# Merged attention posts and a hand-set first batch in a fused RWKV6 and MLP-mixer kernel

## Chip, cores and metric

The kernel runs on one core of one Trainium2 chip. The metric is device time in microseconds (us) of one execution. A kernel's time is the median of several executions; where two kernels are compared, both ran on the same chip in the same rounds. The granted clock is the share of TensorE's full clock that the profile says was granted. All executions that are quoted here count as fast, but for one of the kernel before: at 700.29 us it is 1.6% above that kernel's fastest (689.36), counts as slow and is left out.

## What is computed

Two blocks in float32. The first is a linear-attention recurrence over 768 tokens, for 4 batches of 8 heads of width 48; its output, heads side by side, is the 384-wide input of a mixer with a token MLP (768 to 256 to 768) and a channel MLP (384 to 1536 to 384).

```python
for t in range(S):                                    # attention, per batch and head
    cur = einsum('bhd,bhe->bhde', u[None] * kt, vt)
    y[:, :, t] = einsum('bhd,bhde->bhe', rt, state + cur)
    state = wt[:, :, :, None] * state + einsum('bhd,bhe->bhde', kt, vt)
# mixer
h  = maximum(xt @ w_tok1, 0) @ w_tok2                 # xt: tokens last
u  = x + h.transpose(0, 2, 1)
h2 = maximum(u @ w_ch1, 0) @ w_ch2
return u + h2
```

The four weight matrices arrive as float64, and the kernel itself turns them into float32 on VectorE.

## The kernel before

A batch is three *units* of 256 tokens, a unit two *chunks* of 128. A unit's attention has two halves. `levels` builds the token-by-token weights within 64 tokens in six doubling steps (on TensorE a *gram* of 32 products, which the trace shows as 64 instructions, then *joins* of k, r and w on VectorE and *picks* of the wanted results on VectorE or ScalarE). `post` carries the state: transposes of k, products kv, a state update on VectorE, then y. The *mixer* of a batch is token products (`hidden`, `back`), transposes (`turn`) and, per segment of 256 tokens, `up` and `down` products. Attention of batch n+1 is woven into the mixer of batch n: `woven` mixes lists of pieces in proportion to their estimated costs. During the mixer of batch 0 all weights still have to be converted.

```python
def emit(pieces):                       # the scheduler may reorder what is emitted
    for _, f in pieces:
        f()
...
def convert(dst, src):                  # one piece of float64 weights, six VectorE steps in a chain
    sp.dma_start(d64..., src)           # d64: 2 buffers
    act.activation(size, hi, AF.Abs)
    dve.tensor_scalar(cut, hi, ...)
    dve.scalar_tensor_tensor(cut, hi, ..., cut)
    dve.tensor_scalar(scale, cut, ...)
    dve.scalar_tensor_tensor(low, lo, ..., low)        # low is scale
    dve.tensor_add(low, low, cut)
    dve.scalar_tensor_tensor(dst, size, NORMAL, low, ...)
...
# post(i): for each of the two chunks c of a unit
#   tokens(c): 4 transposes, one copy       carry(c): kv tile of 1 buffer, then the state updates
#   before(c): y from the state              within(c): y from the weights, copy to x
return pieces + [(0.01, lambda: load_rkw(i + 3)), (0.01, lambda: load_v(i + 3))]
...
def up(s, jt):
    if jt == 0:
        zs[s] = mpool.tile([128, NJ, SEG], f32, name="z")          # 2 buffers
    ps = ps_m.tile([128, SEG], f32, name="z_ps", tag="m")          # ps_m: 2 buffers
    ...
def down(s, n, jts=range(NJ)):
    if jts[0] == 0:
        sums[s, n] = ps_m.tile([128, DM], f32, name="h2_ps", tag="m")
    ...
# batch 0
emit(woven(levels(0), levels(1)))
...
emit(woven(levels(2), p0 + p1, to_tok1))
emit(woven(p2[:-4], to_tok2[:2]))
emit(p2[-4:-2] + hiddens[4] + p2[-2:] + hiddens[5])
emit(woven(turned, to_tok2[2:] + to_ch1[:3]))
both = [f for e in zip(ups[0], ups[1]) for f in e]
emit(woven(both, to_ch1[3:] + to_ch2[:6]))
emit(woven(downs[0][:-4], to_ch2[6:]))
pieces = downs[0][-4:] + ups[2] + downs[1] + downs[2]   # then woven with the attention of batch 1
```

Whole units of the next batch may thus be pulled forward by the scheduler into gaps of the weight conversions: nothing but data dependencies and buffers forbids it.

## Time and profile before

| | before |
|---|---|
| median of 3 runs (range) | 690.79 us (689.36 to 692.17) |
| span of the profiled run, mean granted clock | 685.6 us, 0.978 |
| last state add of batch 0 (VectorE) | 76.94 us |
| last weight ready (start of the last conversion's last operation, plus its length) | 183.91 us |
| first token product of batch 1, 2, 3 (TensorE) | 254.76, 411.83, 566.82 us |

The last three rows are markers that I read off the engines' timelines, each from one profiled execution. That execution lay up to 3.2 us from its kernel's median (here 687.6 us against 690.79), so a difference of 2 or 3 us between markers of two kernels shows nothing. I call the last weight's time **W** and the first token product of batch 1 **B1**. The lines on what bounds the kernel are in the prediction. The following were not shown there: what VectorE waited for in the first 190 us of the kernel before (total us, times, longest us).

```profile
DVE k L250 <- PE gram L225: 8.2, 11, 1.5
DVE k L250 <- DMA w<-in_rkw_dram: 5.2, 1, 5.2
DVE state L306 <- PE kv_ps L296: 3.0, 2, 2.4
```

No wait of a conversion is among them, and the longest wait of any kind is 5.2 us.

### The profile page before, as it was taken

The page shows a single profiled execution, that of the slowest core. Times are in us where ns is not written, and L with a number is a line of the kernel's source. Part 1 is how long each engine was busy: PE and PEld are TensorE (multiplying, and loading weights), DVE is VectorE, ACT ScalarE, POOL GpSimd, SP SyncE. Part 2 cuts the span into 40 slices and gives each one's busy share as a digit, 9 for nine tenths or more (in the row PEclk, how much of TensorE's full clock was granted, in tenths as well). Part 3 has the DMA queues.
Part 4 walks back from the last instruction along what each step waited for, and adds up shares of the span by engine and source line. Part 5 has one row for each costly group of instructions (what it writes and reads, how often), then busy time and mean ns, then how long its engine had stood idle before and what let it go on. Part 6 is the DMA issues. An engine that isn't in the chain of part 4 may idle for free.

```text
span 685.6 us, 18835 instructions
## 1 busy us (share of the span) xinstructions
PE 641.6 (94%) x8584; PEld 466.9 (68%) x8584; DVE 293.1 (43%) x585; ACT 194.8 (28%) x489; POOL 7.2 (1%) x32
## 2 busy tenths in 40 slices
PE   3889998996799999999999999999999999999998
PEld 3877656863586666788677656788677655786854
DVE  5998899998821435442242305442132211000000
ACT  7144533441242123432321303432211201220200
POOL 3000000000000000000000000000000000000000
PEclk9997898998899999999999999999999999999999
DMA  9244544332202131110210312000000000000000
GB/s 345 69 107 132 146 140 126 124 115 71 70 25 81 36 95 48 25 25 5 80 35 3 94 35 60 2 2 2 13 13 2 25 12 12 1 0 12 12 16 31
DMA packets 16111, 38.56 MB, mean 56 GB/s; under 512 B 2176, under 2 KB 8320, under 8 KB 16032
## 3 DMA queue, kind: packets, MB, share of 16 engines
q1 hardware_dynamic: 15888, 37.36, 17.9%
q8 instruction: 67, 1.10, 0.7%
q14 instruction: 12, 0.10, 0.0%
q10 hardware_dynamic: 144, 0.00, 0.0%
HBM read 32.64 MB, written 4.72 MB: 54 GB/s over the span
## 4 chain that ended last, share of the span: by engine, by line
PE 87%; DVE 9%; issue 2%; ACT 1%; DMA 1%; SPq 0%; DVEq 0%; ACTq 0%
PE z_ps L375 29%; PE h_ps L384 28%; PE gram L225 9%; PE h_ps L353 5%; PE h_ps L360 5%; PE y_ps L331 4%; PE kv_ps L296 2%; PE y_ps L318 2%; DVE r L251 1%; DVE k L250 1%; PE kT_ps L284 1%; PE gram L211 1%; PE xT_ps L367 1%; DVE at L217 1%; DMA w<-in_rkw_dram 1%
## 5 line engine op out<-in xcount | busy, mean ns | idle before, releaser
L375 PE MATMUL z_ps<-xT,wch 128*128 128x256 f32 x864 | 203.2, 389 | 3.5 <-DVE wch L161 3.0
L384 PE MATMUL h_ps<-wch,z 128*128 128x384 f32 x576 | 198.6, 498 | 3.7 <-DVE wch L161 3.5
L375 PEld LDWEIGHTS z_ps<-xT,wch 128*128 128x128 f32 x864 | 161.4, 192 | 28.4 <-DVE wch L161 3.2
L384 PEld LDWEIGHTS h_ps<-wch,z 128*128 128x128 f32 x576 | 107.9, 192 | 73.1 <-DVE wch L161 3.7
L377 ACT ACTIVATE z<-z_ps 128x256 f32<-128x256 f32 x144 | 55.1, 383 | 177.3 <-PE z_ps L375 177.2
L225 PEld LDWEIGHTS gram<-r,k 48*64 48x64 f32 x3840 | 76.5, 152 | 34.7 <-issue 24.3
L225 PE MATMUL gram<-r,k 48*64 48x32 f32 x3840 | 85.2, 235 | 13.1 <-DVE r L251 8.5
L388 DVE TENSOR_TENSOR o<-x,h_ps 128x384 f32<-128x384 f32 x24 | 13.3, 554 | 181.9 <-PE h_ps L384 181.9
L250 DVE TENSOR_TENSOR k<-k,decay 112x512 f32<-112x512 f32 x36 | 24.9, 691 | 62.2 <-PE gram L225 62.2
L242 ACT COPY at<-gram 16x256 f32<-16x256 f32 (+1 forms) x72 | 31.2, 434 | 44.7 <-PE gram L225 37.3
L250 DVE TENSOR_TENSOR k<-k,w 112x512 f32<-112x512 f32 x36 | 24.8, 688 | 39.6 <-PE gram L225 32.9
L360 PE MATMUL h_ps<-h,wtok 128*128 128x384 f32 x96 | 36.0, 503 | 1.8 <-DVE x L362 1.8
L353 PE MATMUL h_ps<-x,wtok 128*128 128x384 f32 x96 | 37.0, 520 | 0.0
L331 PEld LDWEIGHTS y_ps<-vt,at 64*64 64x64 f32 x768 | 26.2, 142 | 9.9 <-ACT seen L324 6.3
L234 DVE COPY_PREDICATED at<-mask,gram 128x512 f32<-128x512 uint8 x36 | 32.3, 897 | 0.0
L251 DVE TENSOR_TENSOR r<-r,w 112x512 f32<-112x512 f32 x36 | 24.7, 686 | 16.5 <-ACT rp L195 16.5
L331 PE MATMUL y_ps<-vt,at 64*64 64x48 f32 x768 | 29.2, 227 | 2.1 <-ACT seen L324 1.8
L211 PE MATMUL gram<-rp,kp 48*64 48x64 f32 x768 | 20.1, 246 | 11.1 <-ACT kp L199 8.0
L211 PEld LDWEIGHTS gram<-rp,kp 48*64 48x64 f32 x768 | 17.1, 154 | 16.4 <-ACT kp L199 10.4
L217 DVE COPY_PREDICATED at<-mask,gram 128x512 f32<-128x512 uint8 x24 | 16.7, 725 | 25.7 <-PE gram L211 25.4
L155 ACT ACTIVATE size<-d 128x384 f32<-128x384 f32 (+1 forms) x28 | 17.0, 608 | 28.2 <-DMA d<-in_w_ch_dram 13.3
L324 ACT COPY seen<-y_ps 64x2 f32<-64x2 f32 x44 | 6.8, 154 | 63.6 <-PE y_ps L318 63.3
(50 smaller groups left out, 429.1 us busy)
## 6 DMA issues: line engine op xcount, KB each, us to landing
vt<-in_v_dram SPq DMA_DIRECT2D x12, 384.0 KB, 3.9
d<-in_w_ch_dram SPq DMA_DIRECT2D x9, 512.0 KB, 3.6
d<-in_w_ch_dram SPq DMA_DIRECT2D x12, 384.0 KB, 3.0
out_dram<-o SPq DMA_DIRECT2D x24, 192.0 KB, 1.9
w<-in_rkw_dram SPq DMA_DIRECT2D x18, 192.0 KB, 3.5
k<-in_rkw_dram SPq DMA_DIRECT2D x18, 192.0 KB, 3.5
r<-in_rkw_dram SPq DMA_DIRECT2D x18, 192.0 KB, 3.4
r<-in_rkw_dram SPq DMA_DIRECT2D x3, 512.0 KB, 6.1
```

What stands on the lines that cost most here:

```text
L211: pe.matmul(g[cols, q, ts(a, T)], L["kp"][rows, tokens], L["rp"][rows, tokens], start=True, stop=True)
L225: fours(lambda q, j, rows, cols: pe.matmul(g[cols, q, ts(ca, 32)], k_[rows, ds(ca * 128 + j * T, T)], right[rows, ts(2 * ca + j, 32 // b), ...
L234: dve.copy_predicated(out=dst, data=g.rearrange("p q (m b) -> p q m b", b=b), mask=masks[l].rearrange("p x t -> p (x t)").rearrange("p (m ...
L242: act.copy(at[p:p + b, :, :, n * 2 * b + b:(n + 1) * 2 * b], g[p:p + b, :, :, ts(n, b)])
L250: dve.tensor_mul(left, left, wv[:, :, 1].unsqueeze(2).to_broadcast([ROWS, n, b]))
L251: dve.tensor_mul(right, right, wv[:, :, 0].unsqueeze(2).to_broadcast([ROWS, n, b]))
L331: pe.matmul(y[ts(j, T), q, ts(a, D)], at[ts(j, T), q, c * A + a, :], vt[ts(j, T), c, ts(2 * a + q, D)], start=(2 * ch + j == 0 and a == A ...
L353: pe.matmul(sums[i], wtok1[:, c, ts(i, 128)], xs[bt][:, c, :], start=(c == 0), stop=(c == C - 1))
L360: pe.matmul(ps, wtok2[:, i, ts(c, 128)], h1[:, i, :], start=(i == 0), stop=(i == DTOK // 128 - 1))
L375: pe.matmul(ps, wch1[:, m, ts(jt, 128)], xT[:, m, ts(s, SEG)], start=(m == 0), stop=(m == DM // 128 - 1))
L377: act.activation(zs[s][:, jt, :], ps, AF.Relu)
L384: pe.matmul(ps, zs[s][:, jt, ts(n, 128)], wch2[:, jt, :], start=(jt == 0), stop=(jt == NJ - 1))
```

## The change

Its intent: in `post`, both chunks of a unit go through one kv tile and one y tile, so that TensorE's work comes in four blocks instead of eight. In batch 0, the order of TensorE, VectorE, ScalarE and SyncE is set by hand (`fixed=True`), units staggered, with dummy products meant to keep TensorE fast; the three weight-conversion stages are fixed too.

```diff
+    def emit(pieces, fixed=False):
+        for _, f in pieces:
+            ...                         # each TensorE, VectorE, ScalarE, SyncE instruction is put
+            ...                         # behind the last fixed one of its engine
+    emit([(0, make_masks)], fixed=True)
...
-        def carry(c):                  # and tokens(c), before(c), within(c)
+        def carry():                   # and tokens(), update(), before(), within()
-            kv = ps_a.tile([128, 2, 512], f32, name="kv_ps", tag="a")
+            kv = L["kv"] = ps_a.tile([128, 2, 512], f32, name="kv_ps", tag="a")
+            for c in range(UC):
...
-                        pe.matmul(kv[ts(q, P), j, ts(a, D)], L["kT"][ts(j, T), a, ts(q, P)], ...
+                            pe.matmul(kv[ts(q, P), j, ds((c * A + a) * D, D)], L["kT"][ts(j, T), c, a, ts(q, P)], ...
...
-        return pieces + [(0.01, lambda: load_rkw(i + 3)), (0.01, lambda: load_v(i + 3))]
+        return [(1.0, tokens), (1.1, carry), (0.1, update), (1.1, before), (2.2, within),
+                (0.01, lambda: load_rkw(i + 3)), (0.01, lambda: load_v(i + 3))]
...
-    emit(woven(levels(0), levels(1)))
-    emit(woven(levels(2), p0 + p1, to_tok1))
-    emit(woven(p2[:-4], to_tok2[:2]))
-    emit(p2[-4:-2] + hiddens[4] + p2[-2:] + hiddens[5])
+    order = [begin[0], 12, begin[1], a[0], 2, a[1], 2, b[0], 2, a[2], 2, b[1], 2, begin[2], a[3], 2, b[2], 2, c[0], 2,
+             a[4], 2, b[3], 2, c[1], 2, a[5], 2, b[4], 1, c[2], 1, p0[0], b[5], 1, p0[1], p0[2], c[3], 2, p1[0],
+             p0[3], c[4], p0[4], p1[1], p1[2], t1[0], c[5], p1[3], *h[0], p1[4], *h[1], p2[0], t1[1],
+             p2[1], p2[2], *h[2], t1[2], p2[3], *h[3], p2[4], t2[0], t2[1], *h[4], *h[5]]
+    emit([(0.4 * e, lambda e=e: busy(e)) if isinstance(e, int) else e for e in order], fixed=True)
...
-            emit(woven(turned, to_tok2[2:] + to_ch1[:3]))
+            emit(woven(turned, to_tok2[2:] + to_ch1[:3]) + p0[5:] + p1[5:] + p2[5:], fixed=True)
-            emit(woven(both, to_ch1[3:] + to_ch2[:6]))
-            emit(woven(downs[0][:-4], to_ch2[6:]))
+            emit(woven(both, to_ch1[3:] + to_ch2[:6]), fixed=True)
+            emit(woven(downs[0][:-4], to_ch2[6:]), fixed=True)
```

In `order`, `a`, `b`, `c` are the levels of units 0 to 2, `p0` to `p2` their posts, `h` hidden products, `t1`, `t2` token-weight conversions, and an integer is so many dummy products. `p0[5:]` and its like are the loads of units 3 to 5, that is of batch 1. Smaller edits aren't shown: other buffer counts (decay, kT, state), the loads of unit 2 and of v ahead of the hand-set order, mask tiles that share the conversions' `size` buffers, and a tiny first multiply on ScalarE.

## The prediction

Here and in the expectations, TensorE is called warm where it does the same instructions in the shorter time. By the chain of work of the kernel before, 64 gram instructions took 1.97 us at 23.22 us and 1.06 at 301.57; by TensorE's timeline, four transposes of 128x128 took 1.11 us at 38.42 us and 0.66 at 44.09. The granted clock does not tell the two apart there: it is 1.00 from 17 to 34 us. The 356 and 352 of the state update are ns, the means of its two operations.

> **What bounds the kernel now.** I read the page's shares and 40 slices first, then busy time by stage, then what TensorE waited for, then the chain that ended last and VectorE's timeline. First the page: engines, then slices of 17.1 us.
>
> ```profile
> PE 641.6 (94%) x8584; PEld 466.9 (68%) x8584; DVE 293.1 (43%) x585; ACT 194.8 (28%) x489; POOL 7.2 (1%) x32
> ...
> PE   3889998996799999999999999999999999999998
> PEld 3877656863586666788677656788677655786854
> DVE  5998899998821435442242305442132211000000
> ...
> PEclk9997898998899999999999999999999999999999
> ```
>
> The kernel has two regimes. From slice 12 TensorE is full and nothing else matters. In slices 1 to 11 VectorE is nearly full while TensorE has holes and a clock below full. The stage table (us, then busy time of PE, PEld, DVE, ACT, POOL) puts numbers to it:
>
> ```profile
> 7.00:186.00 179.00, 151.21 (x2895) 116.74 (x2895) 162.21 (x329) 69.83 (x170) 0.33 (x3) 0.91 0.41 126
> 186.00:255.00 69.00, 67.65 (x907) 48.19 (x908) 20.94 (x46) 19.17 (x51) 0.33 (x3) 1.00 0.22 62
> 255.00:412.00 157.00, 155.99 (x2211) 111.97 (x2211) 53.06 (x102) 45.24 (x118) 0.22 (x2) 1.00 0.14 39
> 412.00:569.00 157.00, 155.42 (x2151) 111.49 (x2152) 49.29 (x96) 39.43 (x103) 0.00 (x0) 1.00 0.05 16
> ```
>
> From 7 to 186 us VectorE is busy 91%, TensorE idle for 27.8 us and granted 0.91 of its clock. From 186 us on TensorE is idle only 1 to 2 us per 157 us batch. So waits inside posts are worth very little later; the lost time is early. TensorE's waits agree (total us, times, longest):
>
> ```profile
> PE gram L225 <- DVE r L251: 8.5, 7, 2.6
> PE gram L211 <- ACT kp L199: 8.0, 1, 8.0
> PE h_ps L384 <- DVE wch L161: 3.5, 2, 2.1
> PE z_ps L375 <- DVE wch L161: 3.0, 2, 2.3
> ...
> PE y_ps L331 <- ACT seen L324: 1.8, 4, 1.1
> ```
>
> The two waits that a post owns (for seen, and 1.4 us for state) are 3.2 us in all. In the chain of work, the same 64 gram instructions take twice as long early, and the first token matmul of a batch marks the batches:
>
> ```profile
> 23.22 1.97 PE gram L225 x64
> ...
> 254.84 0.84 PE h_ps L353 x2
> ...
> 301.57 1.06 PE gram L225 x64
> ...
> 411.90 0.84 PE h_ps L353 x2
> ```
>
> So batch 1's mixer begins at 254.8 and a full batch takes 411.9 - 254.8 = 157.1 us. VectorE's timeline shows one weight conversion from first to first operation, and the end of the last one:
>
> ```profile
> 112.12 0.42 DVE L156 TENSOR_SCALAR cut<-d 128x512 uint32<-128x512 uint32 x1
> ...
> 115.90 0.42 DVE L156 TENSOR_SCALAR cut<-d 128x512 uint32<-128x512 uint32 x1
> ...
> 183.36 0.55 DVE L161 SCALAR_TENSOR_TENSOR wch<-size,scale 128x384 f32<-128x384 f32 x1
> ```
>
> A 512-wide conversion alone is 3.78 us; the same view gives 3.1 for a 384-wide one (131.01 to 134.12). The last weight is ready at about 184 us only because VectorE has by then done most of the levels of the second batch's first two units as well: w products and joins of unit 3 run from 70 us on, between conversions.
>
> [...] the trace has 356 and 352 for the state update; the change keeps the number and width of these, so it saves no VectorE work there. [...]
>
> **The change, part by part.**
> *Start.* Twelve dummy products (about 0.43 us each warm, from 15.54 us for 72 of 256 columns[...]) run before the first data at 8 us, then 29 more between the early levels. They occupy TensorE where it waits for VectorE[...]. Masks go first on VectorE instead of between the first joins. Cost about 16 us of TensorE in a VectorE-bound stretch: zero if it stays so.
> *First batch on VectorE*, in issue spacing (0.605 us for 512-wide operations without a wait between them, 0.34, 0.20, 0.13 for the shrinking products): a unit is 3.2 + 2.65 + 2.0 + 1.95 + 1.3 + 1.3 = 12.4 us, three 37.2. State updates as dependent chains of about 0.4 us: 8.3. Two of three token conversions before the last update: 7.6. Start 7.2. Sum 60.3. Waits by the new order: 3 while the first unit runs alone, 1.5 for the first carry, 1.2 and 2.7 around unit 1's carry and 1 for unit 2's: 9.4. So unit 2's update ends at about **70 us** (before: its last state add is at 76.9).
> *Conversions.* Left then: one of 512 and four of 384 for the token weights, nine of 512, twelve of 384, and six x additions: 10*3.78 + 16*3.1 + 3 = 90 us, now in fixed order with no level of batch 1 between. Last weight at about **160 us**, not 184. This is the heart of it: the units of batch 1 no longer delay the weights.
> *TensorE meanwhile* does 8 us of token back products, 2.5 of transposes, 31 of the first two up segments, 10 of down: 52 us in 80, so it waits some 25 us here. Its last fixed instruction needs the eighth down weight, four conversions (12.4 us) before the last: 160 - 12 + 1 = about 150 us. From then the third up segment (15.5 us) fills the rest.
> *From 150 us* TensorE has left: 5.2 + 3*15.5 = 51.7 of the mixer and the whole attention of batch 1. A unit is 6*1.06 of grams, 2.1 + 1.2 + 1.2 of y and kv, 1.0 of transposes: 12.0, three 36. Sum 87.7. How much a mixture loses: a batch is 36 + 111 (46.6 up, 46.5 down, 15.9 token, 2.5 transposes) = 147.5 and takes 157.1, a factor of 1.065. 87.7*1.065 = 93. Batch 1's mixer starts at about **243**, 12 us earlier.
> *Posts later.* Four TensorE pieces per unit instead of eight. A piece that cuts into a run costs about 0.2 us (six z products alone take 1.49, 72 together 15.54, that is 1.30 for six). Three units times four cuts is 2.4 us per batch at most; against it, y now waits for four updates instead of two with one buffer. I choose 1.5 us for each of the two later mixed batches: 3.
> Sum: 690.8 - 12 - 3 = **676 us**.
>
> **Rivals.** (a) *VectorE waits more in fixed order than I count.* A piece that waits blocks all behind it. For: 9.4 us of waits are a hand count, each gram-join-gram turn could add 0.5 us, and a conversion costs 3.78 in fixed order against about 3.3 with other work between. At double the waits the last weight is at 170 and the gain is near 4: about 686. (b) *Batch 1's attention becomes the bound.* Nothing of it starts before about 150 us; 18 levels at about 3 us in turn plus posts is some 70 us against 93 of TensorE work. It should fit, since units overlap. If it doesn't, 5 us are lost: 681. (c) *Warm TensorE and fewer cuts are worth more.* If VectorE's early waits vanish since grams take 1.06 us, not 1.97, and merged posts give the full 2.4 per batch, the first batch ends 8 us sooner and the result is about 664. (d) *Nothing changes, as the posts were hidden anyway.* The 3.2 us of waits speak for it as far as posts alone go; the order of the weights speaks against it as a whole: about 689.
>
> **Range and chances.** 676 is 2.1% under 690.8; the 2% line is 677.0, so the middle sits on it. Errors of ±10 us come from the hand count of waits; (a) and (c) lie on both sides. Range **664 to 688**; faster by over 2% **0.53**, within 2% **0.43**, slower **0.04** (only if the fixed order blocks badly).
>
> **What would show it.** In the new profile: early runs of 64 grams near 1.06 us; the last state add of batch 0 near 70; the last wch conversion near 160 with nearly no levels of unit 3 before it; waits of z_ps and h_ps on wch growing to 20 us or more; the first L353-type product of batch 1 near 243; batches of about 155.5 after that. It is wrong if the weights end no earlier than 175, if TensorE idles after the weights waiting for joins or state, or if the batches after it change by more than 3 us.

## The result and the profile after

The changed kernel took **713.44 us** (median of 4, 710.35 to 715.11) against 690.79 (689.36 to 692.17, its three fast runs; with the slow one a median of 691.48) for the kernel before on the same chip. The ratio is 1.0323, with a 95% interval of 1.0271 to 1.0375: slower. Ratios here are the mean time of one kernel's fast runs over that of the other's of the same rounds, so not quite the ratio of the medians quoted. Results were correct. The profiled run took 710.35 us, with a span of 708.4 us.

The page of the changed kernel, engines and then slices of 17.7 us:

```profile
PE 650.9 (92%) x8666; PEld 469.6 (66%) x8666; DVE 300.9 (42%) x587; ACT 190.6 (27%) x470; POOL 7.5 (1%) x32
...
PE   8887874788789999999999999999999999899998
...
DVE  6885583799966452634224212623223120100000
```

In the prediction's page VectorE had nines or eights in slices 2 to 10. Here slices 4 to 7 fall to 5, 5, 8 and 3, and TensorE has a 4 in slice 7. Busy time by stage (us, then PE, PEld, DVE, ACT, POOL, then clock, DMA share, GB/s):

```profile
7.00:186.00 179.00, 135.80 (x2043) 97.52 (x2042) 136.87 (x267) 54.44 (x131) 0.84 (x5) 0.90 0.40 121
186.00:255.00 69.00, 64.34 (x1463) 48.86 (x1464) 44.65 (x87) 25.37 (x68) 0.22 (x2) 0.98 0.18 52
```

From 7 to 186 us VectorE did 136.87 us of work instead of 162.21, and TensorE 135.80 instead of 151.21, dummies included. What was not done there follows: from 186 to 255 us VectorE has 44.65 us instead of 20.94. VectorE's waits in the first 190 us name what stopped it:

```profile
DVE cut L174 <- DMA d<-in_w_ch_dram: 14.1, 1, 14.1
DVE wtok L179 <- ACT size L173: 6.6, 2, 6.3
...
DVE state L333 <- PE kv_ps L316: 4.6, 1, 4.6
DVE mask L147 <- POOL size L141: 4.0, 3, 3.5
```

One wait of 14.1 us for a weight load is new, and larger than the whole predicted gain. The last operation of the last conversion, and the first token product of batch 1, from the timelines of VectorE and TensorE:

```profile
186.79 0.56 DVE L179 SCALAR_TENSOR_TENSOR wch<-size,scale 128x384 f32<-128x384 f32 x1
...
278.98 0.91 PE L382 MATMUL h_ps<-x,wtok 128*128 128x384 f32 x2
```

The markers, before and after:

| | before | after | predicted |
|---|---|---|---|
| last state add of batch 0 | 76.94 | 81.17 | about 70 |
| W, last weight ready | 183.91 | 187.35 | about 160 |
| B1, first token product of batch 1 | 254.76 | 278.98 | about 243 |
| B1 − W | 70.9 | 91.6 | 83 |
| the next two batches | 157.07, 154.99 | 155.96, 154.70 | 1.5 less each |

### The profile page after: what moved, and what is told of

It reads as the page before. It is cut to its first block, busy times and chain, and to the rows that moved or that the text cites. A ratio compares the mean times of both kernels' runs of the same rounds, so it can differ in the third digit from the quotient of the medians.

```text
span 708.4 us, 18967 instructions
## 1 busy us (share of the span) xinstructions
PE 650.9 (92%) x8666; PEld 469.6 (66%) x8666; DVE 300.9 (42%) x587; ACT 190.6 (27%) x470; POOL 7.5 (1%) x32
## 3 DMA queue, kind: packets, MB, share of 16 engines
q8 instruction: 68, 1.11, 0.7%
## 4 chain that ended last, share of the span: by engine, by line
PE 76%; DVE 15%; DMA 5%; ACT 2%; issue 2%; SPq 0%; DVEq 0%; ACTq 0%
PE h_ps L413 25%; PE z_ps L404 22%; PE gram L243 8%; PE h_ps L382 4%; PE h_ps L389 4%; PE y_ps L364 4%; PE busy L445 2%; DMA d<-in_w_ch_dram 2%; PE kv_ps L316 2%; DVE k L268 2%; DVE cut L175 2%; DVE scale L177 2%; PE y_ps L347 2%; PE kT_ps L306 1%; PE gram L229 1%
## 5 line engine op out<-in xcount | busy, mean ns | idle before, releaser
L413 PE MATMUL h_ps<-wch,z 128*128 128x384 f32 x576 | 195.2, 492 | 6.6 <-DVE wch L179 6.2
L404 PEld LDWEIGHTS z_ps<-xT,wch 128*128 128x128 f32 x864 | 163.8, 194 | 42.7 <-ACT z L406 15.5
L243 PEld LDWEIGHTS gram<-r,k 48*64 48x64 f32 x3840 | 64.3, 136 | 28.2 <-issue 20.2
L243 PE MATMUL gram<-r,k 48*64 48x32 f32 x3840 | 71.5, 221 | 6.3 <-DVE r L269 2.9
L389 PE MATMUL h_ps<-h,wtok 128*128 128x384 f32 x96 | 37.8, 520 | 5.5 <-ACT xT L397 1.7
L389 PEld LDWEIGHTS h_ps<-h,wtok 128*128 128x128 f32 x96 | 16.9, 194 | 17.2 <-DVE x L391 2.5
L367 ACT COPY x<-y_ps 128x384 f32<-128x384 f32 x24 | 11.5, 480 | 54.9 <-PE y_ps L364 54.9
L445 PE MATMUL busy<-wtok 128*128 128x256 f32 x82 | 24.9, 439 | 1.3 <-DVE wtok L447 1.3
L382 PEld LDWEIGHTS h_ps<-x,wtok 128*128 128x128 f32 x96 | 17.6, 195 | 12.7 <-DVE wtok L179 2.6
```

Of the source, the lines that this page charges most:

```text
L243: fours(lambda q, j, rows, cols: pe.matmul(g[cols, q, ts(ca, 32)], k_[rows, ds(ca * 128 + j * T, T)], right[rows, ts(2 * ca + j, 32 // b), ...
L382: pe.matmul(sums[i], wtok1[:, c, ts(i, 128)], xs[bt][:, c, :], start=(c == 0), stop=(c == C - 1))
L389: pe.matmul(ps, wtok2[:, i, ts(c, 128)], h1[:, i, :], start=(i == 0), stop=(i == DTOK // 128 - 1))
L404: pe.matmul(ps, wch1[:, m, ts(jt, 128)], xT[:, m, ts(s, SEG)], start=(m == 0), stop=(m == DM // 128 - 1))
L413: pe.matmul(ps, zs[s][:, jt, ts(n, 128)], wch2[:, jt, :], start=(jt == 0), stop=(jt == NJ - 1))
L445: pe.matmul(ps, wtok2[:, 0, :128], wtok2[:, 0, :256], start=True, stop=True)
```

## The experiments

**What is in dispute.** Theory: the burst of unit loads sits in front of the channel-weight loads in SyncE's fixed order and starves VectorE. Rivals: the posts themselves are slower; the dummy products cost time; fixing the weight stage costs time, as it keeps batch 1's levels out of the gaps; the hand-set start is at fault. SyncE's timeline of the changed kernel, where a row is a group of loads with the time that they took to issue:

```profile
102.85 0.33 SPq L167 DMA_DIRECT2D d<-in_w_ch_dram  x1
103.23 0.89 SPq L112 DMA_DIRECT2D r<-in_rkw_dram  x2
...
119.39 0.38 SPq L119 DMA_DIRECT2D vt<-in_v_dram  x1
120.83 1.23 SPq L167 DMA_DIRECT2D d<-in_w_ch_dram  x2
```

Between two weight loads, at 102.85 and 120.83, lie all loads of three units: for each six of 192 KB (48 rows of 1,024 floats) and one of 384 KB, 4.7 MB in all. VectorE's timeline shows what that does:

```profile
112.55 0.69 DVE L179 SCALAR_TENSOR_TENSOR wch<-size,scale 128x512 f32<-128x512 f32 x1
...
127.35 0.43 DVE L174 TENSOR_SCALAR cut<-d 128x512 uint32<-128x512 uint32 x1 [14.11 <-DMA d<-in_w_ch_dram]
```

The conversions stop at 113.2 and resume when the load issued at 120.83 has landed, 6.50 us later by the chain of waits. From 106 to 126 us the DMA engines were busy throughout, at 223 to 381 GB/s.

All runs in one table; "before" is the median of the kernel before (fast runs), markers are from the profiled run. The four calls ran on different chips, so across calls compare the ratios.

| kernel | median us (range) | before | ratio (95%) | W | B1 | B1 − W |
|---|---|---|---|---|---|---|
| the change | 713.44 (710.35 to 715.11) | 690.79 | 1.0323 (1.0271 to 1.0375) | 187.35 | 278.98 | 91.6 |
| e1 loads late | 705.49 (704.37 to 708.12) | 692.12 | 1.0184 (1.0123 to 1.0244) | 173.66 | 274.99 | 101.3 |
| e2 posts only | 694.17 (691.45 to 696.24) | 692.12 | 1.0013 (0.9951 to 1.0074) | 189.45 | 260.28 | 70.8 |
| e3 no dummies | 719.41 (717.47 to 720.82) | 692.12 | 1.0379 (1.0306 to 1.0451) | 195.17 | 287.78 | 92.6 |
| e4 loads late, t1 early | 709.61 (702.97 to 711.28) | 692.12 | 1.0220 (1.0145 to 1.0295) | 178.61 | 280.07 | 101.5 |
| e5 loads early, weights free | 714.92 (711.76 to 716.92) | 694.64 | 1.0302 (1.0238 to 1.0367) | 217.91 | 283.58 | 65.7 |
| e6 loads early | 701.58 (699.24 to 706.47) | 694.64 | 1.0129 (1.0046 to 1.0212) | 177.12 | 269.63 | 92.5 |
| e7 old start, weights fixed | 697.79 (697.67 to 702.82) | 694.64 | 1.0077 (1.0011 to 1.0143) | 173.65 | 266.49 | 92.8 |
| e8 before with dummies | 704.61 (701.93 to 707.63) | 694.64 | 1.0159 (1.0093 to 1.0225) | 202.64 | 273.10 | 70.5 |
| e12 old start, conversions first | 700.17 (698.33 to 700.58) | 694.70 | 1.0089 (1.0028 to 1.0149) | 174.24 | 267.16 | 92.9 |
| e13 hand start mended | 708.12 (701.73 to 708.44) | 694.70 | 1.0178 (1.0092 to 1.0263) | 184.38 | 276.95 | 92.6 |
| e14 old start, fixed, staggered | 689.03 (687.69 to 692.45) | 693.82 | 0.9940 (0.9889 to 0.9992) | 163.48 | 256.38 | 92.9 |
| e15 posts, staggered | 682.98 (681.65 to 684.94) | 693.82 | 0.9839 (0.9798 to 0.9880) | 174.35 | 251.15 | 76.8 |

Numbers 9 to 11 are missing: they gave z a third buffer, meant to let the third up segment start early. The pool that holds z would then take 52.5 kB of each partition, and the build refuses it, as only 40.7 kB are left for that pool.

### First call: the loads, the posts, the dummies

**e1** moves the burst behind the last conversion.

```diff
-            emit(woven(turned, to_tok2[2:] + to_ch1[:3]) + p0[5:] + p1[5:] + p2[5:], fixed=True)
+            emit(woven(turned, to_tok2[2:] + to_ch1[:3]), fixed=True)
...
-            emit(woven(downs[0][:-4], to_ch2[6:]), fixed=True)
+            emit(woven(downs[0][:-4], to_ch2[6:]) + p0[5:] + p1[5:] + p2[5:], fixed=True)
```

> The changed kernel with the loads of units 3 to 5 issued behind the last weight load instead of ahead of the fourth channel load. Theory 'burst': the 14.1 us that VectorE waited for the channel weights behind 2.9 MB of unit data is lost time on the path; the last weight should be ready at about 173 us instead of 187.4, batch 1's mixer should start near 265 instead of 279.0, and the time should be about 699 us (ratio to before 1.012). Rival 'the burst is hidden, the late start of batch 1's attention is what counts': the last weight comes earlier but the attention then waits for its own data, and the time stays at 710 or more.

(The 2.9 MB in that text is an error of mine: it is 4.7 MB, as worked out above.) Measured: the 14.1 us wait for channel weights is gone and W comes 13.7 us earlier, at 173.66. B1 comes only 4 us earlier. The unit loads are now issued between 166.65 and 181.94 us, after the weights, and the grams of batch 1 start later than the weights allow. The time is between the two that I had named, and clearly under the change's, as the intervals of the ratios don't overlap. So the burst did delay the weights by the length of its wait, and the far end of the queue is no place for it either.

**e2** takes the posts alone into the kernel before (the prediction's rival (d), as far as posts go).

```diff
 # the kernel before, with post() of the change, and
-    p1[4:4] = hiddens[0] + hiddens[1]
-    p2[4:4] = hiddens[2] + hiddens[3]
+    p1[3:3] = hiddens[0] + hiddens[1]
+    p2[3:3] = hiddens[2] + hiddens[3]
-    emit(woven(p2[:-4], to_tok2[:2]))
-    emit(p2[-4:-2] + hiddens[4] + p2[-2:] + hiddens[5])
+    emit(woven(p2[:-3], to_tok2[:2]))
+    emit(p2[-3:] + hiddens[4] + hiddens[5])
```

> The kernel before with only the merged posts (one kv and one y tile per unit, updates as their own piece); start and order as before. Theory 'order': the posts are not what made the changed kernel slow, so this is at or a little under before: 686 to 691 us, batches 156 to 155 us long. Rival 'posts': waiting for four state updates with one buffer costs in the first batch, so this is slower than before by 5 us or more.

Measured: the same as before, 1.0013. The posts don't cause the loss. In the profiled run B1 is 5.5 us later than before while the later batches are shorter, 155.97 and 154.70 us.

**e3** takes the dummy products out of the hand order.

```diff
-    emit([(0.4 * e, lambda e=e: busy(e)) if isinstance(e, int) else e for e in order], fixed=True)
+    emit([e for e in order if not isinstance(e, int)], fixed=True)
```

> The changed kernel without the 41 dummy products. If they keep TensorE warm and the early path depends on gram time: early runs of 64 grams go back to about 2 us, the first units end up to 8 us later, time 714 to 722. Rival 'dummies are in the way': VectorE waited 16 us for grams, part of it behind dummies; without them it waits less and the time falls to 705 to 711.

Measured: 719.41 us, ratio 1.0379 against 1.0323 with dummies. The dummies are not what costs; taking them out points to a loss of about half a per cent (the intervals overlap). Early runs of 64 gram instructions take 1.93 us instead of 1.14, although the granted clock from 7 to 40 us is 1.00 in both profiles, so there the durations decide; the last state add is 5.3 us later (86.48), W 7.8 and B1 8.8.

**e4** is e1 with the second token conversion moved ahead of unit 1's y.

```diff
-             p0[3], c[4], p0[4], p1[1], p1[2], t1[0], c[5], p1[3], *h[0], p1[4], *h[1], p2[0], t1[1],
+             p0[3], c[4], p0[4], p1[1], p1[2], t1[0], c[5], t1[1], p1[3], *h[0], p1[4], *h[1], p2[0],
```

> As e1, and the second token conversion stands right behind unit 2's last level, ahead of unit 1's y. Theory 'fixed order blocks': the 6.3 us that VectorE waited at 72 us for the ScalarE step of that conversion, stuck behind copies of unit 1 and 2, go away: last weight near 167 us, time about 693 (6 us under e1). Rival: the wait only moves to unit 2's carry or the token products, and e4 equals e1 within 2 us.

Measured: 709.61 us, from 702.97 to 711.28. Inconclusive: in the profiled run the mean granted clock was 0.957 (0.973 in e1), and VectorE was late well ahead of the edited place, which it reaches only after 60 us: the last product of the first unit's decays (w_chunk) starts at 46.05 us instead of 41.23 in the changed kernel. The last state add was later too (85.14).

### Second call: where the loads should be, and what fixing the weights costs

**e6** puts each unit's loads in the hand order as soon as the unit's buffers are free.

```diff
-             p0[3], c[4], p0[4], p1[1], p1[2], t1[0], c[5], p1[3], *h[0], p1[4], *h[1], p2[0], t1[1],
+             p0[3], c[4], p0[4], p1[1], p1[2], t1[0], c[5], *p0[5:], p1[3], *h[0], p1[4], *h[1], p2[0], t1[1], *p1[5:],
-             p2[1], p2[2], *h[2], t1[2], p2[3], *h[3], p2[4], t2[0], t2[1], *h[4], *h[5]]
+             p2[1], p2[2], *h[2], t1[2], p2[3], *h[3], p2[4], t2[0], t2[1], *p2[5:], *h[4], *h[5]]
-            emit(woven(turned, to_tok2[2:] + to_ch1[:3]) + p0[5:] + p1[5:] + p2[5:], fixed=True)
+            emit(woven(turned, to_tok2[2:] + to_ch1[:3]), fixed=True)
```

> The changed kernel with each unit's next loads issued inside the hand-set order, soon after the unit's y is done, instead of as one burst. The weight stage stays fixed. Theory 'fixed weight stage': only the 14 us wait for data goes; the last weight is ready near 173 as in the run with late loads, batch 1's attention has its data at once, the attention stretch after the last weight shrinks from 101 us to about 92, time about 695 to 699. Rival: early loads hold up the token weights in the same queue, and nothing is gained on the run with late loads (705).

Its last conversion, and the first token product of batch 1, from the timelines of VectorE and TensorE:

```profile
176.56 0.56 DVE L179 SCALAR_TENSOR_TENSOR wch<-size,scale 128x384 f32<-128x384 f32 x1
...
269.63 0.91 PE L382 MATMUL h_ps<-x,wtok 128*128 128x384 f32 x2
```

W comes 10.2 us and B1 9.4 us earlier than in the changed kernel, and the ratio falls from 1.0323 to 1.0129. This is the largest single repair. The wait for channel weights is no longer among VectorE's waits. B1 − W stays at 92.5: what is left to do after the last weight is the same.

**e5** is e6 with the scheduler free in the three weight stages.

```diff
-            emit(woven(turned, to_tok2[2:] + to_ch1[:3]), fixed=True)
+            emit(woven(turned, to_tok2[2:] + to_ch1[:3]))
 # and the same for the two emits after it
```

> As e6, but the three emissions of the weight stage are not fixed, so the scheduler mixes batch 1's levels between the conversions as in the kernel before; the start stays in its hand-set order. Theory 'fixed weight stage': what the change loses is that VectorE and TensorE no longer do batch 1's levels in the gaps of the conversion chains. The last weight comes later than in e6 (195 us or so), yet batch 1's mixer starts near 255 and the time is 684 to 691, 8 us or more under e6. Rival 'hand-set start': if the start is what costs, e5 stays within 3 us of e6.

This contradicted me. I had taken the fixed weight stage for the second cause; freed, it gave 714.92 us (1.0302), worse than e6. The scheduler put the levels of all three units of batch 1 between the conversions: W is 217.91. B1 − W falls to 65.7, since by then that work is done, but W came 40.8 us later and only 26.8 came back. It isn't a clean test, though: from 82 to 218 us the granted clock was 0.80 (0.92 in the kernel before from 82 to 184), and VectorE waited 11.0 us for grams (there 3.9). How much of the late W is the clock's and how much the order's stays open.

**e7** asks the same from the other side: the kernel before with the new posts (e2), with only the weight stages fixed.

```diff
 # e2, with the change's emit(), and
-            emit(woven(turned, to_tok2[2:] + to_ch1[:3]))
+            emit(woven(turned, to_tok2[2:] + to_ch1[:3]), fixed=True)
 # and the same for the two emits after it
```

> The opposite corner: start as in the kernel before (scheduler free, no dummies, unit loads as before) with merged posts, and only the weight stage emitted in fixed order. Theory 'fixed weight stage': last weight earlier than before's 184 us (near 172), but all of batch 1's levels behind it that were not done in the start; time 695 to 705, 5 us or more slower than the run with merged posts only (694). Rival 'hand-set start': this is within 3 us of the merged posts alone, 691 to 697.

Measured: 697.79 us, 1.0077, against 1.0013 for e2. Fixing the weights brings W 15.8 us earlier (189.45 to 173.65), and B1 is still 6.2 us later, since B1 − W grows from 70.8 to 92.8. What the weights gain, batch 1's attention loses. That the whole is slower than e2 isn't shown, as the intervals overlap and the two ran on different chips.

**e8** gives the kernel before the dummies.

```diff
+    busy(12)
-    emit(woven(levels(0), levels(1)))
+    emit(woven(levels(0), levels(1), [(1.0, lambda: busy(2))] * 12))
```

> The kernel before with dummy products in the start (14 ahead of the first grams, the rest between the levels of the first two units), nothing else. If warmth shortens the path: early runs of 64 grams fall from 1.97 to about 1.1 us, VectorE's 8 us of waits for grams shrink by half, time 3 to 6 us under before. If VectorE holds the pace there anyway, the time is within 1 us of before.

Measured: 704.61 us, 1.0159; the last state add is at 84.99 and W at 202.64. The granted clock from 7 to 40 us was 0.74 in its profiled run (1.00 in the kernel before), so the dummies didn't even keep the clock. In that stretch they took 17.0 of TensorE's 31.0 busy us, and up to the last state add VectorE waited 11.2 us for grams, instead of 4.3 in the kernel before. So much of the 8 us by which the state is late was spent behind slow grams and dummies. With a free scheduler they also change the order of everything else, so how much of the loss is the order's stays open.

### Third call: the hand-set start

**e12** is e7 with three conversions ahead of the token back products, meant to close VectorE's longest wait there (13.1 us for `h_ps`).

```diff
-            emit(woven(turned, to_tok2[2:] + to_ch1[:3]), fixed=True)
+            emit((to_tok2[2:] + to_ch1[:3])[:3] + woven(turned, to_ch1[1:3]), fixed=True)
```

> As the run with the old start and the fixed weight stage, but three conversions stand ahead of the first x addition in the fixed order, where VectorE had waited 13.1 us for TensorE (80 to 93 us). Theory 'last weight plus 93 us': in every fixed kernel whose unit data was there in time, batch 1's mixer starts 91.6 to 92.8 us after the last weight, because TensorE has 93 us of work left that cannot start sooner. So three conversions (10 us) earlier move the whole end: last weight near 164, batch 1's mixer near 256, time 686 to 690. Rival 'batch 1's attention chain or the clock decides': the last weight moves, the end moves by less than half of it, time 694 or more.

It missed its aim. That wait shrank to 4.8 us, but VectorE's waits in the first 190 us now have these:

```profile
DVE cut L167 <- DMA d<-in_w_ch_dram: 6.8, 1, 6.8
...
DVE x L384 <- PE h_ps L382: 4.8, 2, 3.0
DVE cut L167 <- DMA d<-in_w_tok_dram: 4.5, 1, 4.5
```

W didn't move (174.24), nor did the time. B1 − W held at 92.9.

**e13** is e6 with two token conversions right behind `c[5]`, to give ScalarE's step time, and with the masks not fixed.

```diff
-             ... t1[0], c[5], *p0[5:], p1[3], *h[0], p1[4], *h[1], p2[0], t1[1], *p1[5:],
+             ... t1[0], c[5], t1[1], t1[2], *p0[5:], p1[3], *h[0], p1[4], *h[1], p2[0], *p1[5:],
-             p2[1], p2[2], *h[2], t1[2], p2[3], ...
+             p2[1], p2[2], *h[2], p2[3], ...
-    emit([(0, make_masks)], fixed=True)
+    emit([(0, make_masks)])
```

> The changed kernel with early unit loads, masks left to the scheduler, and both remaining 512-wide token conversions right behind unit 2's last level, so that VectorE has work while TensorE does the y of unit 1 (before: waits of 8.5 us for ScalarE and 4 us for kv). By the same theory: first join near 7.2 us, last weight 8 to 10 us earlier than in the run with early loads only (177.1), batch 1's mixer near 260, time 691 to 694. Rival: the conversions merely push unit 2's update and the token products later by as much as they gain, and the time stays at 699 to 702.

Inconclusive, and instructive. Three runs took 708.00 to 708.44 us at clocks near 0.957, one took 701.73 at 0.975. In the profiled run (a slow-clock one), four windows from 20 to 36 us look like this one (columns as in the stage table):

```profile
28.00:32.00 4.00, 4.00 (x84) 3.10 (x80) 2.11 (x5) 0.00 (x0) 0.00 (x0) 0.50 0.00 0
```

TensorE is busy for 4.00 of 4.00 us and granted half its clock, for 16 us on end, with runs of 64 gram instructions at 1.93 us. So being busy was not enough for the full clock here. Even at its best run, the mended start only equals e6.

### Fourth call: shorter conversions

e1 to e13 leave two quantities: how early W is, and how much is left after it. **e14** moves W alone. It is e7 with staggered conversions: pieces of at most 384 columns, the last three operations of a piece alternating with the first three of the next, so that no operation follows the one that it depends on.

```diff
+        d64 = wide.tile([128, 2 * n], u32, name="d64", bufs=3)        # was 2
+        cut = wide.tile([128, n], u32, name="cut", bufs=2)            # was 1
...                                    # a yield after each VectorE operation of convert
+    def step(make=None):
+        old, new = (open_.pop() if open_ else None), (make() if make else None)
+        for _ in range(3):
+            for e in (old, new):
+                if e is not None:
+                    next(e)
+        if new is not None:
+            open_.append(new)
```

> The run with the old start and the fixed weight stage, but the weights are converted in 384-wide pieces (256 for the first token weight) whose six operations are interleaved with those of the next piece, so that no operation follows the one it depends on. In fixed order a chain of 384 takes 3.1 us, of which the operations issued back to back need about 2.4. Theory 'last weight plus 92.6 us': 24 channel pieces at 2.45 instead of 71 us of chains bring the last weight from 173.7 to about 161, batch 1's mixer from 266.5 to about 254, and the time to 684 to 688, under both kernels. Rival 'the stretch behind the last weight is set by something else': the last weight moves, batch 1's mixer by less than half as much; 693 or more.

VectorE's timeline of e14, three operations in the staggered stretch and the last three, where nothing is left to alternate with:

```profile
122.45 0.55 DVE L171 TENSOR_TENSOR scale<-scale,cut 128x384 f32<-128x384 f32 x1
122.92 0.55 DVE L163 SCALAR_TENSOR_TENSOR cut<-d,cut 128x384 uint32<-128x384 uint32 x1
123.39 0.55 DVE L173 SCALAR_TENSOR_TENSOR wch<-size,scale 128x384 f32<-128x384 f32 x1
...
161.67 0.56 DVE L169 SCALAR_TENSOR_TENSOR scale<-d,scale 128x384 f32<-128x384 uint32 x1
162.26 0.56 DVE L171 TENSOR_TENSOR scale<-scale,cut 128x384 f32<-128x384 f32 x1
162.92 0.56 DVE L173 SCALAR_TENSOR_TENSOR wch<-size,scale 128x384 f32<-128x384 f32 x1
```

Operations of the same length start 0.47 us apart when they don't depend on each other, and 0.59 to 0.66 apart when they do. A 384-wide piece takes 2.67 us (between the same operation of two pieces, 121.31 and 123.98) instead of 3.1. Against e7, W is 10.2 us earlier, B1 10.1 us, the time about 9. In this pair, W passes on one to one. Not all of W's gain need be the staggering, since e14 also has a third load buffer. The traces divide it: VectorE waited 3.0 us for a token-weight load in e7 and for none in e14, while the channel weights, for which neither waited, take 24 pieces of 2.67 us instead of nine of 3.77 and twelve of 3.11, that is about 7 us less.

**e15** takes the same conversions into e2, where the scheduler is free.

```diff
 # e2, with convert(), step() and conversion() of e14; no emit is fixed
```

> The kernel before with merged posts and the same interleaved conversions, scheduler free everywhere. In the free order other work already fills half of the gaps in the chains, so less is to be had: last weight some 5 us earlier than with merged posts alone (189.5), time 686 to 692. If the scheduler uses the room for batch 1's levels first, the time stays at 692 to 696.

Measured: 682.98 us, 0.9839 (0.9798 to 0.9880). At a 2% line the verdict is unclear, but the interval excludes "no gain": this version beats both kernels. Next to e2 (1.0013) it differs in the conversions alone, their third load buffer included. Its W, 174.35, is later than e14's 163.48, and yet its B1 is 5.2 us earlier, as only 76.8 us are left after it.

## Why the prediction was wrong, step by step

The prediction had the time at 676 and B1 at 243; they are 713.44 and 278.98. The 36 us on B1 divide as: state end 11.5, conversions 15.8, what follows the last weight 8.6. With the posts' 1.6 us less than hoped, 676 becomes about 713.5. That this closes is no proof of the causes below: the three terms are differences of the same markers.

**"Unit 2's update ends at about 70": wrong by 11.5 us.** It ended at 81.5. The lines from VectorE's timeline after:

```profile
9.40 0.69 DVE L268 TENSOR_TENSOR k<-k,w 112x512 f32<-112x512 f32 x1
...
78.55 0.69 DVE L179 SCALAR_TENSOR_TENSOR wtok<-size,scale 128x512 f32<-128x512 f32 x1 [6.27 <-ACT size L173]
...
81.17 0.35 DVE L333 TENSOR_TENSOR state<-state,kv_ps 128x192 f32<-128x192 f32 x1
```

The first join starts at 9.40, not at the 7.2 that I assumed: the masks, now fixed in front of it, wait for GpSimd. That is 2.2 us; in e13, where the masks are free, a join waits 4.9 us for its load instead, as the first one does in the kernel before (5.2 us, start at 7.16). A token conversion waits 6.27 us for its step on ScalarE, which stands in ScalarE's order behind copies of y and kT; I had counted VectorE's and TensorE's order and not ScalarE's. The wait for a carry is 4.62, where I had 2.7. Together 10.4 of the 11.5. The sum of work was right, 53.3 us from the first join on without waits, where I had 53.1. The waits were mis-sized: 18.8 us in all, double my 9.4, which is what rival (a) allowed for.

**"Last weight at about 160": wrong by 27.4 us, of which 11.5 are the step before.** The sum of conversions itself was right: from 81.5 to 187.35 are 105.8 us, less the wait of 14.1 that is 91.7, and I had 90. What failed is the unwritten assumption that a load is always there. I read the fixed order for VectorE and never for SyncE, whose order it sets as well. e6 shows the cause by removing it, e1 does so from the other side.

**"Its last fixed instruction needs the eighth down weight ... From then the third up segment fills the rest": the lead of 10 us doesn't exist.** TensorE's timeline after, with the waits in brackets:

```profile
181.19 1.56 PE L413 MATMUL h_ps<-wch,z 128*128 128x384 f32 x4 [1.55 <-DVE wch L179]
184.30 1.56 PE L413 MATMUL h_ps<-wch,z 128*128 128x384 f32 x4 [1.55 <-DVE wch L179]
...
187.72 1.56 PE L413 MATMUL h_ps<-wch,z 128*128 128x384 f32 x4
...
191.23 1.99 PE L404 MATMUL z_ps<-xT,wch 128*128 128x256 f32 x8 [0.16 <-DVE o L417]
```

TensorE follows the weights one by one, at work 1.56 us of every 3.11, and the third up segment starts only after the last of them. By the code, it must: z has two buffers, both held by the first two segments, and both `ps_m` buffers are held by the two open down sums. So B1 = W + 93, not W + 83. The 93 us that I added up for TensorE were right: seven kernels with the weights fixed and batch 1's data in time (the change, e3, e6, e7, e12, e13, e14) show 91.6 to 92.9, with TensorE busy for 86.4 to 88.6 of them, where I had 87.7. No run shows the buffers' part alone, as the third buffer didn't fit.

**"No level of batch 1 between" is not a gain in itself.** This is the heart of it. In the kernel before, B1 − W is 70.9: between the conversions, the scheduler lets both engines do much of batch 1's attention. Of batch 1's 18 joins of k (six in each unit), 13 start before W in the kernel before and in e2, 10 in e15, all 18 in e5, and at most one in the kernels with the weights fixed. Fixing the stage moves 22 us of that work behind W. Thus W has to come below 254.8 − 92.5 = 162.3 us only to break even. My 160 alone, with the true 93 behind it, gives B1 = 253, a gain under 2 us. e14, with W = 163.48, comes out near even, as it should: B1 is 1.6 us after that of the kernel before, and the ratio 0.9940 (0.9889 to 0.9992). e7 shows the trade with the start unchanged.

**Posts: mechanism right, term too large.** I counted 3 us for two batches; the batches are shorter by 1.11 and 0.29, so 1.4. Alone they don't show in the time (e2).

**The rivals.** (a), more waits in fixed order, was the nearest, and up to the last state add the waits did double; but I sized it at 10 us and didn't look for it on ScalarE and SyncE. A piece that waited did hold up those behind it: while a conversion waited 6.27 us for ScalarE, VectorE started nothing else, and the six state operations behind it, for none of which the profile shows a wait, ran only from 79.16 us on. (b), batch 1's attention as a bound of its own, did not come: the 93 us are TensorE's work, as predicted. (c): most early grams were fast, at 1.06 to 1.14 us instead of 1.97. By e3's profiled run that was worth 8.8 us at B1 within the hand-set order (in time half a per cent, not clear of noise), but no gain over the kernel before came of it. (d) holds for the posts. My 4% for slower was far too small: I had the fixed order only as a source of waits to be doubled, and not as something that can put 4.7 MB ahead of a load that is needed.

**How the loss adds up, by ratios:** posts 1.0013; weight stages fixed as well 1.0077 (e7); the hand-set start as well 1.0129 (e6); the loads where the change has them 1.0323. The first three have overlapping intervals; the last step stands clear. **Left open:** how much of e8's loss is the dummies' and how much the order's; what the hand-set start alone costs; what makes the granted clock fall to 0.50 at about 20 us in e8 and e13; why the free scheduler in e5 prefers levels to weights.

## What to carry to other kernels

When an order is fixed by hand, walk it once for every engine that it binds, the load queue and ScalarE included, and ask at each load how many bytes stand ahead of it: here 4.7 MB ahead of one load held VectorE for 14.1 us. Bringing the last of something forward is only worth what isn't left to do after it: compare both numbers, here W and B1 − W, before and after. And where one engine's chain sets the pace, taking apart the operations that depend on each other was here worth more (0.9839 in e15 against 1.0013 in e2) than reordering everything around it (1.0323). Dummy products that are to keep TensorE fast need the profile as proof: e3 shows early grams at 1.93 us without them and 1.14 with them, but in e8 and e13, which have them, they took 1.93 as well, at a granted clock of 0.50.
